# Seven moves in a hand-written order: three accumulating GpSimd transfers later, four other pieces earlier, and four sums of the last chunk on other engines

## The chip, the cores and the metric

The kernel runs on one core of a Trainium2 chip. The number that counts is the device time of one execution in microseconds (us). Before the change three runs took 835.11, 837.05 and 841.11 us, with a median of 837.05 us.

## What is computed

Attention with a causal window of 64 positions over 8 batches, 8 heads, 576 positions and 64 values a head; its output is the input of a gated network without a bias:

```python
scores = (q @ k.T) / 8, only where 0 <= pos_q - pos_k < 64
x = softmax(scores) @ v                 # 4608 tokens x 512
h = x @ w_in                            # 512 -> 2048
g = h * erf(softplus(h))
out = g @ w_out                         # 2048 -> 512, float32
```

## The kernel before

The 4608 tokens are 36 units of 128 for the attention and 18 chunks of 256 for the network. Everything stays on one core, and stages of several units and chunks overlap: while chunk c is in its second product, chunk c+1 or c+2 is in its first, and later units are in the attention.

**Order.** No scheduler decides anything. A string, PLAN, lists tokens such as `B:17:6:0:v`; a loop at the end of the function calls one small function for each token, and every engine gets its instructions in the order of the tokens. The last letter of many tokens says which engine does the piece: `v` VectorE (DVE), `a` ScalarE (ACT), `g` GpSimd (POOL), `d` an accumulating transfer that GpSimd issues. So moving a token moves its instructions on one engine's queue alone, and the others meet it through semaphores.

**The second product from chunk 7 on** is made of seven products of quadrants in place of eight. The gated values y of a chunk lie in two tiles (y_107 and y_108 in the order below), two quadrants in each. The products are called m = 1, 4, 2, 5, 6, 3, 7. The tokens that the change touches, and those beside them:

- `S:c:m` (part_sum, L949 as a transfer, L951 on VectorE) adds one quadrant to another, 128x1024 float32. `S:c:3:d` adds the quadrant of m = 6 to the quadrant of m = 3, both in y_108, by a transfer of 512 KB.
- `A:c:m:h` (part_hi, L585) casts half h of a quadrant to float16, and `B:c:m:h` (part_lo, L944) writes what the cast lost: float32 quadrant less float16 cast, again as float16. Four buffers serve all products in turn, so a cast waits until the matmuls of an earlier product have read its buffer.
- `P:c:m:h` (8 matmuls, L965) multiplies the cast by both float16 parts of the weights, and `Q:c:m:h` (4 matmuls, L965) multiplies the rest from B.
- `K:c:k` (first_out, L412 on ACT, L414 on DVE) scales a PSUM bank into the output row, `J:c:k` (more_out, L985 and L982 on DVE) adds another bank to it. The banks are then written again by the next P.
- `ph:u:p` (L585) and `r:u:p` (L552) make the same two parts of the attention's exponentials; `m:u:p` (L510) masks scores and takes their maximum; `nb` (L517), `n` (normalize, L573 to L575), `dc` (L750) and `gn` (L756, L758) are small.
- `C` (L831) adds PSUM to the hidden values, `E` copies PSUM (L583 or L585), `M` (L815) are the seven products of the first layer.

Of the kernel before, what the change touches and what calls it, by code (L numbers as in the profile page):

```python
# [18 lines left out]
B, H, S, D = 8, 8, 576, 64  # L19
# [3 lines left out]
P = 128  # L23
# [251 lines left out]
)  # L275

# [800 lines left out]
```

## Time and profile before

| | us |
|---|---|
| median of 3 runs | 837.05 (835.11 to 841.11) |
| the profiled execution | 835.41 |
| its span | 833.3 |
| TensorE busy | 807.2 (97%) |
| VectorE busy | 731.7 (88%) |
| ScalarE busy | 629.7 (76%) |
| GpSimd busy | 358.9 (43%) |
| granted TensorE clock, mean | 0.997 |

Busy time counts an instruction from its start to its end, so that an instruction which is held up in the middle counts as busy all the while. The queue of an engine is in order: what waits holds back all that is behind it. [...]

### The profile page before, as it was taken

How to read it: one execution, taken by the hardware profiler on the slowest of the kernel's cores; microseconds unless marked ns; L12 is line 12 of the kernel's file. 1: busy time of each engine (PE TensorE's matmuls, PEld its weight loads, DVE VectorE, ACT ScalarE, POOL GpSimd, SP SyncE). 2: the span in 40 equal slices, each digit the busy share in tenths (PEclk: the TensorE clock that was granted, in tenths of full speed). 3: DMA queues.
4: the chain of work that ended last, by engine and by line, in shares of the span. 5: the costliest groups of instructions: out<-in, count | busy, mean ns of one | idle time of the engine just before them, and what ended most of it. 6: DMA issues, size and time to landing. Idle time of an engine off the chain costs nothing.

```text
span 833.3 us, 26816 instructions
## 1 busy us (share of the span) xinstructions
PE 807.2 (97%) x11358; PEld 675.1 (81%) x11358; DVE 731.7 (88%) x1629; ACT 629.7 (76%) x962; POOL 358.9 (43%) x366
## 2 busy tenths in 40 slices
PE   7899999999999999999999999999998999999996
PEld 7787767566777667667989999999997989899995
DVE  5899999999989998889898899999898888896775
ACT  3799999987878988887778676767786687565482
POOL 1242363424445562822446736283724461523233
PEclk9999999999999999999999999999999999999998
DMA  9974594571486566451746775937476534412222
GB/s 348 360 287 145 149 260 105 121 170 51 104 180 127 144 126 158 121 135 33 137 89 128 178 141 98 212 85 141 98 123 145 111 78 85 74 41 61 52 53 51
DMA packets 148808, 110.40 MB, mean 132 GB/s; under 512 B 123472, under 2 KB 123856, under 8 KB 148688
## 3 DMA queue, kind: packets, MB, share of 16 engines
q1 hardware_dynamic: 145808, 98.60, 48.4%
q0 software_dynamic: 2736, 9.96, 6.4%
q8 instruction: 89, 1.46, 0.8%
q14 instruction: 31, 0.25, 0.1%
q10 hardware_dynamic: 144, 0.13, 0.0%
HBM read 59.64 MB, written 9.44 MB: 83 GB/s over the span
## 4 chain that ended last, share of the span: by engine, by line
PE 64%; DVE 21%; ACT 6%; issue 4%; DMA 3%; POOL 1%; DVEq 0%; SPq 0%; POOLq 0%; ACTq 0%
PE hp L815 27%; PE o L965 15%; PE o L877 12%; PE s L499 3%; PE av L565 3%; PE hp L771 2%; DVE h L944 2%; DVE y L951 1%; DMA y<-y 1%; DVE sm L510 1%; ACT y L839 1%; DVE y L853 1%; DVE h L831 1%; DMA arena<-w_out 1%; PE o L1004 1%
## 5 line engine op out<-in xcount | busy, mean ns | idle before, releaser
L965 PEld LDWEIGHTS <-h 128*128 128x128 f16 x1632 | 156.5, 98 | 27.1 <-DVE h L944 5.5
L815 PE MATMUL hp<-arena,w 128*128 128x128 f16 x2688 | 161.9, 219 | 0.0
L815 PEld LDWEIGHTS <-w 128*128 128x128 f16 x2688 | 154.6, 98 | 6.5 <-issue 2.1
L815 PE MATMUL hp<-arena 128*128 128x128 f16 x2016 | 120.0, 219 | 0.3 <-DVE h L831 0.2
L815 PEld LDWEIGHTS <-arena 128*128 128x128 f16 x2016 | 114.8, 98 | 4.1 <-issue 1.4
L965 PE MATMUL o<-w,h 128*128 128x256 f16 x912 | 109.6, 273 | 2.4 <-DVE ob L985 0.7
L583 ACT ACTIVATE h<-hp 128x512 f32<-128x512 f32 x104 | 60.6, 585 | 42.8 <-PE hp L815 34.7
L771 PE MATMUL hp<-arena,w 128*128 128x256 f16 (+1 forms) x960 | 89.2, 251 | 2.2 <-DVE w L419 1.6
L771 PEld LDWEIGHTS <-w 128*128 128x128 f16 x960 | 77.7, 98 | 13.2 <-DVE w L419 2.1
L839 ACT ACTIVATE y<-h,c 128x1024 f32<-128x1024 f32 x72 | 80.1, 1142 | 10.2 <-DVE h L831 8.7
L583 ACT ACTIVATE h<-y 128x512 f16<-128x512 f32 x79 | 46.8, 623 | 43.2 <-PE o L965 12.8
L944 DVE TENSOR_TENSOR h<-y,h 128x512 f16<-128x512 f32 x95 | 74.1, 797 | 4.3 <-ACT h L583 2.4
L877 PE MATMUL o<-w,gh 128*128 128x512 f16 x320 | 75.0, 379 | 0.2 <-ACT arena L412 0.2
L944 POOL TENSOR_TENSOR h<-y,h 128x512 f16<-128x512 f32 x41 | 53.3, 1324 | 50.6 <-DVE h L585 16.0
L846 ACT ACTIVATE y<-y 128x1024 f32<-128x1024 f32 x72 | 74.4, 1052 | 0.4
L831 DVE TENSOR_TENSOR h<-hp,h 128x512 f32<-128x512 f32 x84 | 57.6, 686 | 18.9 <-PE hp L815 16.4
L851 DVE SCALAR_TENSOR_TENSOR y<-h,small,y 128x1024 f32<-128x1024 f32 x44 | 58.0, 1331 | 4.7 <-ACT y L846 4.5
L965 PE MATMUL o<-spare,h 128*128 128x256 f16 x460 | 55.7, 274 | 3.2 <-DVE h L944 3.2
L877 PEld LDWEIGHTS <-gh 128*128 128x128 f16 x320 | 30.2, 98 | 32.9 <-issue 0.5
L846 ACT ACT_TABLE_LOAD x39 | 50.0, 1283 | 0.7
L499 PE MATMUL s<-kr,qr 64*64 64x128 f32 x1152 | 41.2, 280 | 6.6 <-DMA kr<-k_in 4.7
L949 POOL DMA_DIRECT2D y<-y x19 | 17.2, 903 | 69.1 <-DVE h L585 14.8
(256 smaller groups left out, 1661.4 us busy)
## 6 DMA issues: line engine op xcount, KB each, us to landing
vr<-v_in SPq DMA_DIRECT2D x36, 520.0 KB, 4.3
kr<-k_in SPq DMA_DIRECT2D x36, 384.0 KB, 4.0
y<-y POOLq DMA_DIRECT2D x19, 512.0 KB, 5.1
qr<-q_in SPq DMA_DIRECT2D x36, 256.0 KB, 3.8
out<-ob SPq DMA_DIRECT2D x33, 256.0 KB, 2.9
w<-w_in SPq DMA_DIRECT2D x4, 1024.0 KB, 8.6
arena<-w_in SPq DMA_DIRECT2D x4, 1024.0 KB, 9.2
arena<-w_out SPq DMA_DIRECT2D x4, 1024.0 KB, 6.0
```

The source lines that it names most:

```text
L499: nc.tensor.matmul(sps[par][t, i, :], qx[rows, i, t], kx[rows, i, W * blk:W * blk + P], start=n == 0, stop=n == len(terms) - 1)
L565: nc.tensor.matmul(avp[t, par, j, :], pt[a][ab(u)][:, HP * par + j, t], vs[b][ab(u)][:, blk, 2 * j + par, :], start=a + b == 0, stop=a == 1)
L583: nc.scalar.activation(dst, src, AF.Copy)
L771: nc.tensor.matmul(hps[pc % 2][:, f, at_t], w1[a][hf][:, cc, fs], xt[b][c % 2][:, cc:2 * NCC:NCC, :][:, at_x, :], start=(n == 0), stop=(n ...
L815: nc.tensor.matmul(bank[:, q, f, :], left(m, a, 2 * hf + q)[:, cc, f * P:(f + 1) * P], xt[b][c % 2][:, slot + cc, :], start=m in (1, 2, 5) ...
L831: nc.vector.tensor_tensor(dst, bank_view(1), dst, op=ALU.add)
L839: nc.scalar.activation(at(yb, g, n), at(hb, g, n), AF.Softplus, scale=st_c[g][:, n:n + 1])
L846: nc.scalar.activation(y, y, AF.Erf)
L851: nc.vector.scalar_tensor_tensor(y, at(hb, g, n), gain(g, n), y, op0=ALU.mult, op1=ALU.mult)
L877: nc.tensor.matmul(ops[j], a[:, f // 2, j, f % 2, :], w2[b][:, hf * GF + n * GF // 2 + f, :], start=n == 0 and f == 0 and a is gh and b == ...
L944: eng_of(eng).tensor_tensor(lo, quadrant(m)[:, 512 * h:512 * (h + 1)], hi, op=ALU.subtract)
L965: nc.tensor.matmul(dst, a[:, at_f], right(m, n, 2 * h + f // 2)[:, f % 2], start=False, stop=f == 3 and (a is lo or n == 1), skip_group_ch ...
```

## The change

Seven edits of PLAN; no function changes. Before, the three transfers stand right after an earlier piece of GpSimd; now they stand behind later ones.

1. Chunk 7: `A:7:3:1:v A:7:3:0:v` come ahead of `n:21`, and `B:7:7:1:v` ahead of `B:7:3:0:v`, all on VectorE.
2. Chunk 8: `J:8:0` (VectorE) comes ahead of `m:26:1`.
3. Chunk 12: `S:12:3:d` (GpSimd) comes after `B:12:6:0:g` and `r:32:0:g`.
4. Chunk 14: `S:14:3:d` comes after `A:14:6:1:g`, `dc:34:g` and `ph:35:1:g`.
5. Chunk 16: `S:16:3:d` comes after `B:16:5:0:g`.
6. Chunk 17, engines: `B:17:6:0`, `B:17:5:0` and `B:17:5:1` go from GpSimd to VectorE, `B:17:7:1` from VectorE to GpSimd.
7. Chunk 17, order: `B:17:5:1` comes ahead of `K:17:1` and `J:17:0`.

Two of the changed lines, those of chunk 17 (the others only move tokens, as listed):

```diff
-    "B:17:6:1:v P:17:6:1 A:17:5:0:a B:17:6:0:g A:17:7:1:a P:17:6:0 B:17:7:1:v Q:17:6:1 B:17:5:0:g Q:17:6:0 P:17:5:0 "
-    "K:17:1:a J:17:0 B:17:5:1:g P:17:7:1 B:17:7:0:g Q:17:7:1 Q:17:5:0 Q:17:5:1 P:17:7:0 K:17:2:a A:17:3:1:v A:17:3:0:a "
+    "B:17:6:1:v P:17:6:1 A:17:5:0:a B:17:6:0:v A:17:7:1:a P:17:6:0 B:17:7:1:g Q:17:6:1 B:17:5:0:v Q:17:6:0 P:17:5:0 "
+    "B:17:5:1:v K:17:1:a J:17:0 P:17:7:1 B:17:7:0:g Q:17:7:1 Q:17:5:0 Q:17:5:1 P:17:7:0 K:17:2:a A:17:3:1:v A:17:3:0:a "
```

The order of TensorE, ScalarE and SyncE is the same in both kernels; only VectorE and GpSimd differ. In the rows below, h_106, kr_85 and kr_86 are buffers that B writes, y_107 and y_108 the gated values, o_117 a PSUM bank, ob the output row.

VectorE at the end, chunk 17 (the L951 row is `S:17:6`, the L985 row `J:17:0`, the L944 rows are B):

```order
 L951 TENSOR_TENSOR y_108<-y_108,y_107 128x1024
 L585 CAST h_106<-y_108 128x512
-L944 TENSOR_TENSOR h_106<-y_108,h_106 128x512
-L944 TENSOR_TENSOR kr_86<-y_107,kr_86 128x512
+L944 TENSOR_TENSOR h_106<-y_108,h_106 128x512 x2
+L944 TENSOR_TENSOR h_106<-y_107,h_106 128x512 x2
 L985 SCALAR_TENSOR_TENSOR ob<-o_117,sg,ob 128x256
 L585 CAST h_106<-y_108 128x512
```

Between `S:17:6` and `J:17:0` VectorE had two sums B and has four. GpSimd at the same place, behind its last two transfers:

```order
 L949 DMA y_107<-y_107 128x1024
 L949 DMA y_108<-y_108 128x1024
-L944 TENSOR_TENSOR h_106<-y_108,h_106 128x512
-L944 TENSOR_TENSOR h_106<-y_107,h_106 128x512 x2
+L944 TENSOR_TENSOR kr_86<-y_107,kr_86 128x512
 L944 TENSOR_TENSOR kr_85<-y_107,kr_85 128x512
 L944 TENSOR_TENSOR h_106<-y_108,h_106 128x512
```

Behind the last transfer GpSimd had four sums in a row and has two, and then a last one that belongs to m = 3. GpSimd in chunk 12 (the L949 row that moves is `S:12:3`, L552 is `r:32:0`, the L585 row is `A:12:7:0`):

```order
 L944 TENSOR_TENSOR h_106<-y_107,h_106 128x512
 L949 DMA y_107<-y_107 128x1024
-L944 TENSOR_TENSOR h_106<-y_108,h_106 128x512
-L949 DMA y_108<-y_108 128x1024
-L944 TENSOR_TENSOR h_106<-y_108,h_106 128x512
+L944 TENSOR_TENSOR h_106<-y_108,h_106 128x512 x2
 L552 TENSOR_TENSOR p_0_98<-sm_95,p_0_97 128x512
+L949 DMA y_108<-y_108 128x1024
 L585 CAST h_106<-y_107 128x512
```

The transfer has gone behind one sum B and one sum of the attention.

## Rows read from the trace of the kernel before

**Rows 1.** The page: busy us (share of the span) and instructions of each engine.
```profile
PE 807.2 (97%) x11358; PEld 675.1 (81%) x11358; DVE 731.7 (88%) x1629; ACT 629.7 (76%) x962; POOL 358.9 (43%) x366
```

**Rows 2.** Timeline of chunk 17: start us, us, engine, line, instruction; idle time before it.
```profile
815.44 0.88 POOL L949 DMA_DIRECT2D y<-y  x1 [8.98 <-DVE h L585]
816.00 3.72 POOL L944 TENSOR_TENSOR h<-y,h 128x512 f16<-128x512 f32 x3
816.74 4.63 DVE L944 TENSOR_TENSOR kr<-y,kr 128x512 f16<-128x512 f32 x1 [0.64 <-ACT kr L583]
818.21 0.47 ACT L412 ACTIVATE ob<-o,sg 128x256 f32<-128x256 f32 x1 [1.50 <-PE o L965]
819.34 1.48 POOL L944 TENSOR_TENSOR kr<-y,kr 128x512 f16<-128x512 f32 x1
821.83 2.62 PE L965 MATMUL o<-w,kr 128*128 128x256 f16 x12 [2.78 <-DVE ob L985]
```

**Rows 3.** Line L944: instructions, minimum/median/maximum ns, first and last start.
```profile
L944 DVE TENSOR_TENSOR h<-y,h x95: 671/685/2403, 405.2 to 827.9; 128x512 f16<-128x512 f32 x95
L944 POOL TENSOR_TENSOR h<-y,h x41: 1144/1163/2135, 404.1 to 827.2; 128x512 f16<-128x512 f32 x41
```

**Rows 4.** Stretches: busy time of each engine, then granted clock, DMA share, GB/s.
```profile
821.80:825.40 3.60, 3.57 (x18) 2.50 (x18) 0.31 (x1) 0.00 (x0) 0.00 (x0) 0.53 0.00 0
628.20:630.10 1.90, 0.09 (x2) 0.05 (x2) 1.90 (x11) 0.02 (x1) 0.06 (x1) 1.00 0.98 195
```

**Rows 5.** Timeline at 467 and at 474 us: single meetings of the two engines.
```profile
467.61 2.18 DVE L419 SCALAR_TENSOR_TENSOR vs<-vr,csc,vs 128x1024 f16<-128x1024 f32 x1
474.58 2.24 POOL L552 TENSOR_TENSOR p<-qk,p 128x512 f16<-128x512 f32 x1 [0.56 <-ACT p L583]
```

**Rows 6.** Timeline of chunk 12.
```profile
624.55 0.86 POOL L949 DMA_DIRECT2D y<-y  x1 [3.97 <-DVE h L944]
625.16 3.40 DVE L585 CAST p<-sm 128x512 f16<-128x512 f32 x1
627.38 0.89 POOL L585 CAST h<-y 128x512 f16<-128x512 f32 x1
630.06 1.05 PE L965 MATMUL o<-spare,h 128*128 128x256 f16 x8 [1.81 <-DVE h L944]
634.24 0.63 ACT L583 ACTIVATE h<-y 128x512 f16<-128x512 f32 x1 [0.66 <-PE o L965]
```

**Rows 7.** Timeline of chunk 14.
```profile
708.17 0.88 POOL L949 DMA_DIRECT2D y<-y  x1 [4.03 <-DVE y L951]
708.61 2.40 DVE L944 TENSOR_TENSOR h<-y,h 128x512 f16<-128x512 f32 x1
709.63 0.83 POOL L585 CAST p<-qk 128x512 f16<-128x512 f32 x1
711.07 3.78 PE L965 MATMUL o<-spare,h 128*128 128x256 f16 x33 [0.61 <-DVE h L944]
712.80 0.63 ACT L583 ACTIVATE h<-y 128x512 f16<-128x512 f32 x1 [4.38 <-DMA y<-y]
715.21 0.63 ACT L583 ACTIVATE h<-y 128x512 f16<-128x512 f32 x1 [0.62 <-PE o L965]
```

**Rows 8.** Timeline of chunk 16.
```profile
787.89 2.07 DVE L944 TENSOR_TENSOR vr<-y,vr 128x512 f16<-128x512 f32 x1
790.02 1.48 PE L965 MATMUL o<-spare,vr 128*128 128x256 f16 x12 [0.34 <-DVE vr L944]
796.00 0.61 POOL L585 CAST vr<-y 128x512 f16<-128x512 f32 x1 [2.02 <-PE o L965]
```

**Rows 9.** Timeline of chunks 7 and 8.
```profile
424.01 1.92 PE L965 MATMUL o<-w,h 128*128 128x256 f16 x16 [0.51 <-DVE h L585]
465.78 5.40 PE L965 MATMUL o<-w,h 128*128 128x256 f16 x48 [0.66 <-DVE ob L985]
```

**Rows 10.** Line L949: from issue to landing of the 19 transfers.
```profile
DMA to landing us min/median/max: 4.5/5.1/7.2
```

42 rows, old and new, of the table PLAN are left out of this document.

## Prediction

> **What bounds the kernel now.** I first read the busy times: TensorE is busy 97% of the span, VectorE 88%, GpSimd 43% [rows 1]. So a change pays only where TensorE stands still, and there is little of that. Next I read the timeline at each of the seven places, for two things: an idle time in front of a TensorE row, and a VectorE row much longer than its kind. They come together. A sum B takes VectorE 0.685 us at the median and GpSimd 1.163 [rows 3]. In chunk 17 one took VectorE 4.63 us, and in that time GpSimd ran four sums without a gap, from 816.00 to 820.82; VectorE ended 0.55 us after GpSimd did [rows 2]. The same is seen in chunk 12 (a cast of 3.40 us; GpSimd ends at 628.27, the cast at 628.56) [rows 6], and sums of 2.40 in chunk 14 [rows 7] and 2.07 in chunk 16 [rows 8] are of the same sort. Each time GpSimd had just issued a transfer for which it had waited, so that the pieces behind it were ready and came in a row. I read this as one resource that either engine holds while it works from SBUF to SBUF, and that GpSimd, once it runs in a row, does not hand over.
>
> Single meetings show the rest [rows 5]. At 467.61 VectorE needed 2.18 us: one GpSimd piece was ahead of it, and then it went on. At 474.58 GpSimd's sum came while VectorE was at work; it took 2.24 us, 1.1 more than a median sum [rows 3]. So whichever engine comes second waits for the piece of the other, and I take it that a waiting GpSimd gets in at the next boundary between two VectorE instructions.
>
> **Chunk 17.** TensorE stands still for 2.78 us, from 819.05, until `J:17:0` has read its bank [rows 2]. It restarts at a granted clock of 0.53 (mean over 3.6 us) [rows 4]. At full clock the same work takes 3.6 × 0.53 = 1.9, so the clock costs another 1.7 us. In chunk 12 an idle time of 1.81 [rows 6] was followed by no fall: its stretch has 1.00 [rows 4].
>
> Now VectorE has four sums and then `J:17:0`. The first ends at 816.1 as before (816.74 less the 0.64 idle) [rows 2]. `B:17:6:0` and `B:17:5:0` follow at 0.6 to 0.7 each until 817.3. The cast for `B:17:7:1` is done at 816.7, since that sum started then [rows 2]; now GpSimd has it, waits at 817.3 and gets in, with `B:17:7:0` right behind. At the pace of the four, (820.82 - 816.00)/4 = 1.2 each, GpSimd is through at 819.7. Then come `B:17:5:1` until 820.3 and `J:17:0` until 820.8 (0.46, from 821.37 to 821.83 before). TensorE goes on at 820.8 in place of 821.83: **1.0 us**. Its idle time is then 1.75, below the 1.81 that cost no clock, so the **1.7** come back too. The bounds: at best `B:17:5:1` gets in ahead of GpSimd and `J:17:0` waits only for `K:17:1` (ends 818.68) [rows 2]; TensorE goes on at 819.2, 2.6 + 1.7 = 4.3. At worst one more sum stands behind GpSimd's two and the clock falls all the same: 0.4. I take 2.7, because the meeting at 474 us is the nearest case. The transfer of this chunk is issued as early as before, so what reads it is not later.
>
> **Chunk 12.** GpSimd's two sums ahead of the transfer start no later than they did, and VectorE's cast stands behind two pieces instead of three: the third took 0.89, from 627.38 [rows 6]. VectorE is free earlier by **0.9 us**, and the 1.81 in front of TensorE at 630.06 shrinks by as much [rows 6]. Bounds: 0 (the third piece comes as early as before) and 1.81. The transfer is issued near 627.3 in place of 624.55. Its reader on ScalarE started at 634.24 [rows 6], so 633.3 now; with the median landing of 5.1 the data are there at 632.4, with the longest, 7.2, at 634.5 [rows 10]. I cost it at nothing; at worst ScalarE waits 1.2.
>
> **Chunk 14.** The three pieces that go ahead of the transfer started some 0.6 behind it (as 816.00 behind 815.44 [rows 2]), at 708.8, and the third ended at 710.46 [rows 7]. The first needs the sum `S:14:6` as the transfer does, so they now start when the transfer did or a little later, at 708.2 to 708.4, and end at 709.7, with less in their way. The VectorE sum behind them then ends at 710.7 in place of 711.0: **0.3** of TensorE's 0.61 [rows 7]. The transfer is issued at 709.7 in place of 708.17, and here its reader already waits for it, 4.38 us until 712.80 [rows 7]. That row moves to 714.3. The cast after it on ScalarE waited for TensorE itself, until 715.21 [rows 7], and takes up most of the 1.5; I add 0 for it. Bounds for the whole place: -3.0 (worked out below) and +0.6.
>
> **Chunk 16.** `B:16:5:0` comes the 0.6 of an issue earlier, and VectorE's sum is through as much earlier (0 to 1.4, its whole excess over 0.68). TensorE waited 0.34 for it [rows 8]: **0.35**. The transfer is issued near 788.6; with the longest landing it is there at 795.8 [rows 10], and its reader on GpSimd started at 796.00 [rows 8]. Covered.
>
> **Chunks 7 and 8.** The casts ahead of `n:21` end TensorE's wait of 0.51 [rows 9]. `n:21` reads PSUM, and I expect it to go on beside a GpSimd sum; VectorE gains less than TensorE: **0.4** (0 to 0.51). `J:8:0` ahead of four masked maxima ends the wait of 0.66 [rows 9], but takes no work off VectorE, and ScalarE's exponentials behind the maxima come 0.5 later. I count half: **0.3** (-0.5 to 0.66).
>
> **Sum.** 2.7 + 0.9 + 0.3 + 0.35 + 0.4 + 0.3 = 4.95 us. Against the profiled execution (835.41, of which 833.3 span) that gives 830.5; it lies 1.6 below the median of the runs, which gives 832.1. I put the forecast between them, at **831**. What a place gains can be lost later where VectorE sets the pace; therefore the idle times themselves (2.78 + 1.7 + 1.81 + 0.61 + 0.34 + 0.51 + 0.66 = 8.4) are the end of the range and not the forecast.
>
> [...]
>
> **Rivals.** A measurement of this kernel can tell about 1% from no change: below 828.7 is faster, above 845.4 slower.
>
> *Given up after every instruction.* The pieces arrive at new moments, and VectorE gets in behind the first GpSimd piece everywhere. Chunk 17: GpSimd from 817.3 to 818.5, then a sum and `J:17:0`, 819.6, so 2.2 + 1.7 = 3.9. Chunk 12: the cast waits for one sum, 1.8. Chunk 14 0.6, chunk 16 0.35, chunks 7 and 8 1.2. Together 7.9, or 827.5 to 829.2; I take 828. For it: 467 us [rows 5]. Against it: the long waits over several pieces.
>
> *Little is left.* The clock falls in chunk 17 in spite of the shorter wait (1.75 is hardly under 1.81), so 1.0 there, and of the rest only 1.0 lasts until the end, because VectorE at 88% sets the pace in between. 2.0 less: 834. It decides where VectorE has no pause between one place and the next.
>
> *The late transfer of chunk 14 holds ScalarE: slower.* Issued at 709.7, it holds the cast of 715.21 as soon as landing takes over 4.2 (715.21 less two ScalarE pieces of 0.63, less 709.7) [rows 7]. With the longest landing, 7.2 [rows 10], its reader starts at 716.9 and that cast at 718.2, 3.0 late, and TensorE waits as long for the product behind it. If besides only 1.0 of chunk 17 is gained and nothing else, the kernel takes 837 + 2 = 839. Against it: this landing took 4.6 (708.17 to 712.80) [rows 7], and of 19 the median is 5.1 [rows 10].
>
> [...]
>
> **Numbers.** Chances: the forecast 0.52, "after every instruction" 0.22, "little is left" 0.18, "late transfer" 0.08. The range of 826.5 to 836.5 takes in the first three with the spread of single runs about them, and leaves out the fourth and the ends. Faster by over 1%: half of the first rival and a little of the forecast, 0.13. Slower by over 1%: 0.02. The same within 1%: 0.85.
>
> **What would show it.** In the profile after: the sums of chunk 17 on VectorE at 0.7 except one of about 3 us; a wait in front of TensorE there of under 1.8, with a clock of 1.00 behind it; in chunk 12 a cast of about 2.5 in place of 3.40; in chunk 14 a reader some 1.5 later than before. I am wrong if a VectorE row of 4 us stands in another place, if the granted clock falls again, or if the waits of TensorE are shorter at the seven places and longer at others.

## The result, and the profile after

The changed kernel took **827.75 us** (median of 20 runs, 825.32 to 838.74); the kernel before, in 20 runs on the same chips, 838.08 (833.57 to 846.24). The ratio is 0.990, with a 95% interval of 0.9868 to 0.9932: 1.0% faster, a little more than the 0.7% that was forecast (831 against 837.05). Here and below the ratio leaves out the few runs in a slower state and is not the quotient of the two medians. The first rival had said 828. The profiled execution took 828.04, of which 826.1 is its span; before it was 835.41 and 833.3.

The busy times, the row that answers to [rows 1]:

```profile
PE 805.6 (98%) x11358; PEld 674.7 (82%) x11358; DVE 725.4 (88%) x1631; ACT 629.4 (76%) x962; POOL 355.1 (43%) x364
```

The work is the same; VectorE is busy for 6.3 us less although it runs two instructions more. What it lost was waiting inside its instructions. Line L944, that of the sums B, says so (minimum/median/maximum ns), beside [rows 3]:

```profile
L944 DVE TENSOR_TENSOR h<-y,h x98: 671/686/1647, 407.2 to 820.7; 128x512 f16<-128x512 f32 x98
L944 POOL TENSOR_TENSOR h<-y,h x38: 1147/1159/1976, 406.1 to 819.9; 128x512 f16<-128x512 f32 x38
```

No sum B on VectorE takes over 1.65 us now; before there were some of 2.07, 2.40 and 4.63, and a cast of 3.40.

**Where the time went.** TensorE runs the same 11,358 matmuls in the same order in both kernels, so the two traces can be laid beside each other: the start of the same matmul, after minus before. No edit bears on TensorE before 424 us, and there the changed one was already 1.97 us late (a group of 24 matmuls starts at 423.97 in place of 422.00); that is one execution against another. At the end it was 7.25 us early. Each step is this difference just behind a place less the one just ahead of it:

| Place | Forecast | Step measured |
|---|---|---|
| Chunk 7 | 0.4 | 0.91 |
| Chunk 8 | 0.3 | 0.82, of which 0.78 is given back by 504 us |
| Chunk 12 | 0.9 | 1.97 |
| Chunk 14 | 0.3 | 0.77 at 711 us, 0.36 at 716, 0.61 at 722, less 0.11 given back at 725: 1.63 |
| Chunk 16 | 0.35 | 0.50 |
| Chunk 17, the wait | 1.0 | 2.52 |
| Chunk 17, the clock | 1.7 | 1.67 |
| Sum | 4.95 | 9.2 (from 1.97 late to 7.25 early) |

The spans of the two traces differ by 7.2 us, that is 9.2 less the 1.97. The medians of the runs differ by 10.3 and the lowest times by 8.3; single times scatter by more than such a difference, for a reason that runs 9 and 10 show.

Chunk 17, the timeline, to be read beside [rows 2]:

```profile
812.34 3.46 DVE L944 TENSOR_TENSOR h<-y,h 128x512 f16<-128x512 f32 x4
812.36 0.88 POOL L949 DMA_DIRECT2D y<-y  x1 [8.92 <-DVE h L585]
...
813.76 3.05 POOL L944 TENSOR_TENSOR kr<-y,kr 128x512 f16<-128x512 f32 x2 [0.52 <-ACT kr L583]
...
815.72 0.47 DVE L985 SCALAR_TENSOR_TENSOR ob<-o,sg,ob 128x256 f32<-128x256 f32 x1
816.25 0.93 PE L965 MATMUL o<-w,kr 128*128 128x256 f16 x7 [0.27 <-DVE ob L985]
```

VectorE's four sums take 3.46 us in all, and the longest of them 1.65 (the maximum in the rows of L944): it met one sum of GpSimd and went on between GpSimd's two. These end at 816.81, 1.0 us after VectorE's row. GpSimd has a pause of 0.52 between the transfer and the first sum, since that sum now waits for a cast on ScalarE. TensorE waits 0.27 in place of 2.78. The stretch behind it (busy time of PE, PEld, DVE, ACT, POOL, then TensorE's granted clock as a share of full speed, DMA share, GB/s), beside [rows 4]:

```profile
816.20:822.60 6.40, 6.27 (x56) 5.37 (x55) 2.07 (x4) 1.21 (x2) 1.77 (x2) 1.00 0.20 66
```

The granted clock stays at 1.00, where it had been 0.53.

Chunk 12, beside [rows 6]:

```profile
626.08 1.16 POOL L944 TENSOR_TENSOR h<-y,h 128x512 f16<-128x512 f32 x1 [4.44 <-ACT h L583]
626.21 1.31 DVE L585 CAST p<-sm 128x512 f16<-128x512 f32 x1
...
627.21 1.33 POOL L552 TENSOR_TENSOR p<-sm,p 128x512 f16<-128x512 f32 x1
...
628.49 0.86 POOL L949 DMA_DIRECT2D y<-y  x1
...
630.94 0.50 PE L965 MATMUL o<-spare,h 128*128 128x256 f16 x3 [0.75 <-DVE h L944]
```

The cast meets the first of two GpSimd sums and gets in between them: 1.31 us in place of 3.40. The wait of 1.81 is gone; a wait of 0.74 stood behind it before as well, where there is one of 0.75 now.

Chunk 14, beside [rows 7]:

```profile
708.15 0.68 DVE L944 TENSOR_TENSOR h<-y,h 128x512 f16<-128x512 f32 x1
...
709.39 0.88 POOL L949 DMA_DIRECT2D y<-y  x1
...
714.02 0.63 ACT L583 ACTIVATE h<-y 128x512 f16<-128x512 f32 x1 [6.47 <-DVE h L585]
```

The sum of 2.40 us now takes 0.68. The transfer is issued 1.2 us later than before and its reader on ScalarE starts 1.2 later; TensorE stands still nowhere for it.

In chunk 16 VectorE's sum went from 2.07 [rows 8] to 1.45. In chunk 7 the 0.51 in front of TensorE is gone [rows 9], and so is a second wait that the forecast did not look at, 0.24 for a VectorE sum B at 426.18. Chunk 8 has a new short wait of ScalarE on VectorE, whose row that feeds the exponentials stands behind a GpSimd sum:

```profile
466.47 1.16 POOL L944 TENSOR_TENSOR h<-y,h 128x512 f16<-128x512 f32 x1 [1.61 <-ACT h L583]
...
466.68 0.98 DVE L517 TENSOR_SCALAR small<-small 128x8 f32<-128x8 f32 x1
...
467.69 0.40 ACT L543 ACTIVATE sm<-sm,small 128x128 f32<-128x128 f32 x1 [1.29 <-DVE small L517]
```

That this wait is what gave the 0.78 back was not tried.

### The profile page after: what moved, and what is told of

Read it like the earlier page. It is cut to its first block, busy times and chain, and to the rows that moved or that the text cites. A ratio compares the mean times of both kernels' runs of the same rounds, so it can differ in the third digit from the quotient of the medians.

```text
span 826.1 us, 26816 instructions
## 1 busy us (share of the span) xinstructions
PE 805.6 (98%) x11358; PEld 674.7 (82%) x11358; DVE 725.4 (88%) x1631; ACT 629.4 (76%) x962; POOL 355.1 (43%) x364
## 5 line engine op out<-in xcount | busy, mean ns | idle before, releaser
L839 ACT ACTIVATE y<-h,c 128x1024 f32<-128x1024 f32 x72 | 80.0, 1141 | 10.3 <-DVE h L831 9.4
L944 DVE TENSOR_TENSOR h<-y,h 128x512 f16<-128x512 f32 x98 | 74.7, 782 | 4.0 <-ACT h L583 2.8
L944 POOL TENSOR_TENSOR h<-y,h 128x512 f16<-128x512 f32 x38 | 48.5, 1280 | 49.8 <-ACT h L583 19.8
L543 ACT ACTIVATE sm<-sm,small 128x128 f32<-128x128 f32 x124 | 39.0, 389 | 6.7 <-POOL small L517 5.1
```

What stands on the lines that cost most here:

```text
L543: nc.scalar.activation(s[:, j, :], s[:, j, :], AF.Exp, bias=nmx[u % 2][:, HP * par + j:HP * par + j + 1], scale=0.125)
L839: nc.scalar.activation(at(yb, g, n), at(hb, g, n), AF.Softplus, scale=st_c[g][:, n:n + 1])
L944: eng_of(eng).tensor_tensor(lo, quadrant(m)[:, 512 * h:512 * (h + 1)], hi, op=ALU.subtract)
```

## The experiments

The two theories ahead of the runs: by the forecast, GpSimd never hands over once it runs in a row; by the other, the engines take turns after each instruction, except for GpSimd's pieces straight behind a transfer that GpSimd itself issued. The second came from the trace of before: its four VectorE rows that took over 1.1 us more than the median of their kind (3.40, 2.40, 2.07, 4.63 [rows 2, 6 to 8]) are four that stood behind such a transfer. The 2.07 of chunk 16 fits both theories, though: behind that transfer GpSimd ran a single sum, from 787.96 to 789.41, and VectorE's ended 0.55 later. Lines in the variants of the whole kernel are ten lower than in the profiles above (L934 for L944, L939 for L949).

**1. The transfer of chunk 17 moved, nothing else.** The kernel before, with the transfer behind the three sums:

```diff
-P:17:5:1 S:17:3:d K:17:0:a ... J:17:0 B:17:5:1:g P:17:7:1
+P:17:5:1 K:17:0:a ... J:17:0 B:17:5:1:g S:17:3:d P:17:7:1
```

> The kernel before, with one token moved: the last transfer S:17:3 goes behind GpSimd's three sums B:17:6:0, B:17:5:0 and B:17:5:1 (only B:17:7:0 stays behind it); all sums stay on their engines. Theory 1 (the one recorded: GpSimd, once it runs in a row, does not hand over): VectorE's B:17:7:1 still waits for the row, a VectorE row of 3 us or more, TensorE's wait in front of P:17:7:1 over 1.5 us. Theory 2 (VectorE gets in after each GpSimd piece, except in a row straight behind a transfer): a VectorE row of at most 1.7 us, a wait of TensorE under 0.7 us, clock 1.00 behind it, and the TensorE matmuls from there some 4 us earlier, relative to the place before, than in the kernel before. The time is then about 4 us lower, 0.5%.

It took 839.78 us against 835.72 (ratio 1.0013, interval 0.9967 to 1.0059): no gain. The timeline:

```profile
824.94 4.01 POOL L934 TENSOR_TENSOR h<-y,h 128x512 f16<-128x512 f32 x3 [9.30 <-ACT h L573]
...
825.92 0.90 DVE L934 TENSOR_TENSOR kr<-y,kr 128x512 f16<-128x512 f32 x1 [0.66 <-ACT kr L573]
...
828.40 1.47 PE L955 MATMUL o<-w,kr 128*128 128x256 f16 x12 [0.21 <-DVE ob L975]
...
834.05 0.39 PE L955 MATMUL o<-w,h 128*128 128x256 f16 x2 [1.99 <-DVE h L575]
```

The same sum that had taken 4.63 us takes 0.90, beside the same three GpSimd sums, and the wait of 2.78 is 0.21: without the transfer in front of them the engines take turns. About 4.2 us were won there (2.57 of the wait, 1.67 of the clock), but the transfer's data came late, TensorE stood 1.99 us for them and the clock fell once more (granted 0.90 in the mean from 832 to 836 us; from the start of the last 24 matmuls to the end of the span 7.75 us, 6.28 in run 5, some 1.5 more); some 3.5 were given back. The second theory held there (0.90 for 4.63), the expected gain in time is a miss.

**2. The changed kernel with a sum behind the transfer again.**

```diff
-S:17:3:d K:17:0:a ... J:17:0 P:17:7:1 B:17:7:0:g Q:17:7:1
+S:17:3:d B:17:7:0:g K:17:0:a ... J:17:0 P:17:7:1 Q:17:7:1
```

> The changed kernel with one token moved: B:17:7:0 (its cast long done) stands straight behind the last transfer, ahead of B:17:7:1. Theory 2: the two GpSimd sums run in a row from about 0.56 us behind the issue, and one VectorE sum waits for both: a VectorE row of about 2.5 to 3 us where the changed kernel has 1.65 at most. Rival (every GpSimd piece hands over, the transfer has no part in it): no VectorE row there over 1.7 us.

One run took 829.12 us. VectorE's four sums and GpSimd's two in chunk 17:

```profile
L934 DVE TENSOR_TENSOR h<-y,h x4: 677/686/3146, 811.7 to 816.0; 128x512 f16<-128x512 f32 x4
```

```profile
812.29 2.60 POOL L934 TENSOR_TENSOR kr<-y,kr 128x512 f16<-128x512 f32 x2
...
815.51 1.48 PE L955 MATMUL o<-spare,h 128*128 128x256 f16 x12 [1.49 <-DVE h L934]
```

Here GpSimd has no pause behind the transfer, and one VectorE sum waits for both sums (3.15 us; 1.65 in the changed kernel). TensorE now stands 1.49 us for the sum, and by the starts of the same matmuls it is 1.60 us later behind this place than the changed kernel, as measured from ahead of it.

**3. The two engines alone.** A small kernel (it leaves out the whole computation): VectorE runs 12 sums while GpSimd runs four, with something different in front of GpSimd's; each case three times. Four of its six cases:

```diff
+gsum(0, early); gsum(1..3, ga)                               # plain
+gpsimd.dma_start(big0, big1, accum_op=add); gsum(0..3, ga)   # transfer in front
+gpsimd.dma_start(big0, big1); gsum(0..3, ga)                 # plain copy in front
+gpsimd.dma_start(..., accum_op=add); gsum(0, late); gsum(1..3, ga)   # and a wait of ~2 us
```

> A kernel of its own that leaves out the whole computation and measures only how the two engines meet. VectorE runs 12 sums of the form of B (128x512, float32 less float32 to float16) in a row; beside it GpSimd runs four such sums, in six cases, three times each: nothing in front of them; an accumulating transfer of 512 KB from GpSimd straight in front; a plain copy from GpSimd straight in front; the copy issued by SyncE; an accumulating transfer and then a wait of about 2 us before the four; one sum and then the transfer. Theory 1: in all cases with four sums one VectorE sum waits for all of them, 4 us or more. Theory 2: only in the cases with a GpSimd transfer straight in front (accumulating or plain) is there a VectorE row of 4 us or more; in the others no row over 1.9 us, several of about 1.8 in turn. Theory 3 (only accumulating transfers do it): the plain copy behaves as without a transfer.

The durations of VectorE's sums (L33) in the first round of the first three cases, in this order, and in the fourth the first sum of GpSimd (L36):

```profile
L33 DVE TENSOR_TENSOR vo<-va,vb x12: 678/680/1744, 8.1 to 18.7; 128x512 f16<-128x512 f32 x12
...
L33 DVE TENSOR_TENSOR vo<-va,vb x12: 677/678/5767, 20.4 to 32.1; 128x512 f16<-128x512 f32 x12
...
L33 DVE TENSOR_TENSOR vo<-va,vb x12: 676/678/5948, 33.8 to 45.7; 128x512 f16<-128x512 f32 x12
...
L36 POOL TENSOR_TENSOR go<-late,gb x1: 5159/5159/5159, 63.1 to 63.1; 128x512 f16<-128x512 f32 x1
```

Plain, no VectorE sum takes over 1.76 us in any round: a meeting costs it 1.08 at most over the 0.68 of a sum that meets nothing, less than one GpSimd sum (1.25 behind VectorE's row in the fourth case). Straight behind the accumulating transfer one VectorE sum takes 5.77 (5.68 and 5.72 in the other two rounds): it waits for all four. A plain copy issued by GpSimd did the same once in three (5.95; 1.76 and 1.80 in the other rounds). The two cases not shown are as the plain one: behind a copy issued by SyncE, and with the transfer behind GpSimd's sum in place of ahead of it, no VectorE sum takes over 1.76. In the fourth case it is the other way round: GpSimd's sum took 5.16 and ended 1.1 us after VectorE had no more work (VectorE's 12 sums took 0.69 at most). That was expected by neither theory.

Chunks 12 and 17 after the change are like the plain case (1.74 in the round shown): the cast took 1.31 and the longest sum 1.65. In the 5.77, several instructions of GpSimd ran while one of VectorE waited, in the 5.16 several of VectorE while one of GpSimd did; what lets an engine keep on like this, the run does not show.

**4. Is it the wait that costs the clock?** The kernel before, with 24 matmuls that nobody reads put into TensorE's wait:

```diff
-J:17:0 B:17:5:1:g P:17:7:1
+J:17:0 B:17:5:1:g kb:24 P:17:7:1
```

> The kernel before, with 24 matmuls of 128 columns into a hidden bank that is no longer read, put in front of P:17:7:1 on TensorE; they do no part of the computation and fill some 2.4 of the 2.78 us for which TensorE stands still. If the fall of the clock follows from the standstill, the clock stays at 1.00 behind it and the TensorE work from P:17:7:1 to the last matmul (7.96 us before) takes 6.3 us or less, 1.65 us gained at the end. If the clock falls for another reason, it is 0.5 again for 3.4 us and nothing is gained.

```profile
818.58 1.55 PE L998 MATMUL hp<-one,ident 128*128 128x128 bf16 x24
...
821.50 0.71 PE L955 MATMUL o<-w,kr 128*128 128x256 f16 x5 [1.37 <-DVE ob L975]
```

The wait is 1.37 and a filled stretch; the granted clock is 1.00 throughout, and the work from there to the end of the last matmul takes 6.27 us in place of 7.94: 1.67. So the fall belongs to the standstill, and its price is 1.67 us, as the forecast had it. One run took 833.47.

**5 and 6. Chunk 17 alone, and all but chunk 17.** The kernel before with the edits of chunk 17, and the changed kernel without them:

```diff
-B:17:6:0:g ... B:17:7:1:v ... B:17:5:0:g ... J:17:0 B:17:5:1:g
+B:17:6:0:v ... B:17:7:1:g ... B:17:5:0:v ... B:17:5:1:v K:17:1:a J:17:0
```

> The kernel before with the two edits of chunk 17 alone (engines of four sums, B:17:5:1 ahead of J:17:0). Theory 2 (VectorE gets in after each GpSimd piece unless the row follows straight behind a transfer): no VectorE row over 1.7 us there, a wait in front of P:17:7:1 of about 0.3, no fall of the clock, and the end 4.2 us earlier relative to the place before it: ratio near 0.995. Theory 1 (the sizes recorded): 2.7 us, ratio 0.997, a wait of about 1.75.

> The changed kernel without the two edits of chunk 17: chunks 7, 8, 12, 14 and 16 as changed. Theory 2: VectorE rows of at most 1.5 us in chunks 12, 14 and 16, TensorE's matmuls 0.9 earlier behind chunk 7, 1.9 behind chunk 12, 1.7 behind chunk 14, 0.4 behind chunk 16, nothing left of chunk 8; together 4.9 us before chunk 17, where the row of 4.6 us and the fall of the clock are as in the kernel before. Ratio near 0.994. Theory 1 (the sizes recorded): 2.25 us, ratio 0.997.

Chunk 17 alone: 834.01 against 838.68, ratio 0.9957 (0.9919 to 0.9996). All but chunk 17: 830.75, ratio 0.9897 (0.9859 to 0.9936). TensorE's waits in the two, first chunk 17 alone, then all but it:

```profile
629.45 1.05 PE L955 MATMUL o<-spare,h 128*128 128x256 f16 x8 [1.81 <-DVE h L934]
...
819.33 1.47 PE L955 MATMUL o<-w,kr 128*128 128x256 f16 x12 [0.28 <-DVE ob L975]
```

```profile
817.17 4.60 DVE L934 TENSOR_TENSOR kr<-y,kr 128x512 f16<-128x512 f32 x1 [0.68 <-ACT kr L573]
...
822.22 2.72 PE L955 MATMUL o<-w,kr 128*128 128x256 f16 x12 [2.78 <-DVE ob L975]
```

Each half removes its own waits and leaves the other's. In the traces chunk 17 is worth 2.50 and 1.67 for the clock, 4.2 in all; 0.59 was lost just ahead of it, where ScalarE and VectorE waited longer for an earlier transfer (7.3 us to landing, 6.7 in the trace of before). The others show the steps of the table again (0.91, 0.82 with 0.45 given back, 1.97, 1.63, 0.50), 5.4 in all. In time the halves are 4.7 and 7.9 by the medians, together more than the 10.3 of the whole change, and all but chunk 17 did better than the 0.994 that was expected. The 5.4 is 0.9936, the very end of that half's interval; why its runs were faster still stays open.

**7. Can more be had?** The changed kernel with two VectorE pieces earlier:

```diff
-B:12:6:1:v P:12:6:1 ... pk:33:2:v Q:12:6:1 B:12:5:1:v lk:35
+B:12:6:1:v B:12:5:1:v P:12:6:1 ... pk:33:2:v Q:12:6:1 lk:35
-B:17:5:1:v K:17:1:a J:17:0 P:17:7:1
+K:17:1:a J:17:0 B:17:5:1:v P:17:7:1
```

> The changed kernel with two more moves on VectorE: B:12:5:1 straight behind B:12:6:1 (ahead of C:26:2 and a maximum), and J:17:0 ahead of B:17:5:1. If the two waits that the changed kernel still has there (0.75 at 630.2 us and 0.27 at 816.0) hang on these two instructions, both go to 0.1 or less and the kernel takes 1.0 us less than the changed one, ratio to the kernel before near 0.988. Rival: C:26:2, now 0.7 later, holds ScalarE's softplus and TensorE waits later instead; then nothing is gained.

831.86 us (826.36 to 837.79), ratio to before 0.9891 (0.9849 to 0.9933): not to be told from the changed kernel, and the 1.0 us that was expected did not come. The 0.75 of chunk 12 became 0.39, but 0.48 was given back by 638 us. In chunk 17 `J:17:0` now waits for ScalarE, which waits for TensorE:

```profile
814.71 0.48 DVE L975 SCALAR_TENSOR_TENSOR ob<-o,sg,ob 128x256 f32<-128x256 f32 x1 [1.40 <-ACT ob L402]
...
815.25 1.47 PE L955 MATMUL o<-w,kr 128*128 128x256 f16 x12 [0.21 <-DVE ob L975]
```

0.21 in place of 0.27: nothing is left there.

**8. What makes the row behind a transfer.** The small kernel again (it leaves out the whole computation): 18 sums on VectorE, and on GpSimd two sums that are released by the last of k casts on ScalarE (0.65 us each), with and without a transfer in front.

```diff
+scalar.activation(late, mark) x k;  gpsimd.dma_start(..., accum_op=add) or nothing;  gsum(0..1, late);  vsum(0..17)
```

> A kernel of its own that leaves out the whole computation: 18 VectorE sums in a row beside two GpSimd sums, which ScalarE releases after 1, 2, 3, 4, 6 or 9 casts of 0.6 us, with and without an accumulating GpSimd transfer in front (2 times each). Theory 2a: the transfer matters only if the GpSimd sums follow without a pause; then one VectorE sum waits for both (over 2.5 us), and with a pause the engines take turns (rows of 1.7 to 1.8). Theory 2b (from the case with a pause in the first kernel of this kind, where a GpSimd sum behind a transfer took 5.16 us): behind a transfer the engines do not take turns at all; the one that is at work keeps on until it pauses, so that with a pause it is GpSimd's first sum that waits, until VectorE's row ends. Without a transfer they take turns in both theories.

VectorE's sums for k = 1 with and without the transfer, and GpSimd's for k = 4 with it:

```profile
L33 DVE TENSOR_TENSOR vo<-va,vb x18: 676/677/3608, 8.1 to 21.2; 128x512 f16<-128x512 f32 x18
...
L33 DVE TENSOR_TENSOR vo<-va,vb x18: 676/678/1751, 22.9 to 35.3; 128x512 f16<-128x512 f32 x18
...
L36 POOL TENSOR_TENSOR go<-late,gb x2: 1252/4942/8632, 96.4 to 105.0; 128x512 f16<-128x512 f32 x2
```

With k = 1 GpSimd's first sum starts 0.8 us after the start of the transfer's issue (0.6 in the second round), and one VectorE sum waits for both sums (3.61, and 3.24); without the transfer they take turns. With k = 2, where the sum starts 1.0 after it (0.9), and with k = 3 they take turns in either case: a short pause behind the transfer is enough. With k = 4, 6 and 9 GpSimd arrives 3.3 us or more after VectorE's row began, and its first sum ends 1.1 or 1.2 us behind the end of that row (with k = 4 it takes 8.63 us with the transfer and 8.71 without it). So the second surprise of run 3 has nothing to do with the transfer.

**9 and 10. The two terms that were too small, undone one by one.** The changed kernel with the transfer of chunk 14, and of chunk 12, back where it was:

```diff
-B:14:5:0:v Q:14:2:1 ... ph:35:1:g S:14:3:d P:14:5:1
+S:14:3:d B:14:5:0:v Q:14:2:1 ... ph:35:1:g P:14:5:1
-B:12:5:0:v Q:12:2:1 ... r:32:0:g S:12:3:d C:26:2
+S:12:3:d B:12:5:0:v Q:12:2:1 ... r:32:0:g C:26:2
```

> The changed kernel with the edit of chunk 14 undone: the accumulating transfer S:14:3 stands again straight behind S:14:6, ahead of the three pieces of GpSimd. Theory (behind a transfer GpSimd's ready pieces run as one row): the VectorE sum there takes 2.2 to 2.6 us again in place of 0.7, TensorE stands about 0.6 us in front of the matmul that reads it and some 0.4 twice within the next 11 us, and the same matmul of TensorE starts 1.7 us later than in the changed kernel from there on. Rival (the size in the forecast): only the first wait belongs to this edit, the two later ones hung on the order further ahead; 0.3 to 0.6 us later. Second rival (the transfer that was moved back costs its reader): the cast of chunk 14 on ScalarE that reads it had been 1.2 us late, so undoing the edit gains something at 715 us; under 0.3 us later in all.

> The changed kernel with the edit of chunk 12 undone: the accumulating transfer S:12:3 stands again ahead of GpSimd's sums B:12:6:0 and r:32:0. Theory: VectorE's cast waits for the row behind the transfer, 3.2 to 3.6 us in place of 1.31, TensorE stands 1.6 to 2.0 us in front of the matmul that the changed kernel started without a wait, and is 1.9 us later than in the changed kernel behind it. Rival (the forecast's rule, by which the cast stands behind two pieces in the one order and three in the other): 0.9 us later.

Chunk 14 undone:

```profile
717.08 0.87 POOL L939 DMA_DIRECT2D y<-y  x1 [4.03 <-DVE y L941]
717.52 2.40 DVE L934 TENSOR_TENSOR h<-y,h 128x512 f16<-128x512 f32 x1
...
719.98 3.78 PE L955 MATMUL o<-spare,h 128*128 128x256 f16 x33 [0.60 <-DVE h L934]
...
724.63 0.96 PE L555 MATMUL av<-vs,pt 128*64 128x65 f16 x47 [0.40 <-DVE vs L409]
...
730.94 0.28 PE L955 MATMUL o<-w,h 128*128 128x256 f16 x1 [0.44 <-POOL h L934]
```

The sum is back at 2.40, and with it three waits of TensorE, not one. Against the changed kernel the same matmuls start 0.77, then 0.36, then 0.61 us later, and 0.11 comes back behind them: 1.63. Chunk 12 undone:

```profile
628.61 3.40 DVE L575 CAST p<-sm 128x512 f16<-128x512 f32 x1
...
633.51 1.05 PE L955 MATMUL o<-spare,h 128*128 128x256 f16 x8 [1.81 <-DVE h L934]
```

1.97 us later. Both as the theory had it; the rivals fall.

The single times of these two (839.33 and 832.31) say little: in both, TensorE also stood still near 510 us, long before the place of the edit. For chunk 14 undone:

```profile
502.31 0.87 POOL L939 DMA_DIRECT2D y<-y  x1 [5.21 <-DVE cdiag L444]
...
516.06 0.63 ACT L573 ACTIVATE h<-y 128x512 f16<-128x512 f32 x1 [7.00 <-DMA y<-y]
...
517.31 1.01 PE L955 MATMUL o<-w,h 128*128 128x256 f16 x4 [7.01 <-ACT ob L402]
```

That transfer landed after 13.7 us. Four of the ten traces of the whole kernel have such a standstill there (4.68, 3.49, 7.01 and 3.15 us; longest landings of 11.9, 10.1, 13.7 and 10.3), and the other six, those of before and of the changed kernel among them, have none (at most 7.3). Run 1, whose program is that of before up to chunk 17, has it too, so it comes and goes from one execution to another. The clock falls behind it: in run 6, with a wait of 3.49, the 32 matmuls behind took 5.32 us, where 48 took 5.40 in the trace of before. In all it adds up to 10 us: the span of run 9 is 11.4 longer than that of the changed kernel (837.5 and 826.1), of which the edit has 1.63. So steps of a microsecond are read here from the starts of the same matmul, not from single times.

## Why the prediction came out as it did

The sign was right, and so was the place where the time was sought: waits inside VectorE's instructions. The sizes were not: 9.2 us came in the traces for the 4.95 of the sum. The time lies in the range all the same, because the range was made wide enough for the first rival too, and the measured 827.75 is that rival's 828, not the forecast's 831. That much is luck. The terms were too small, mostly because of one step.

**The step that failed** is "GpSimd, once it runs in a row, does not hand over". Where a row was seen not to hand over, it followed a GpSimd transfer without a pause (runs 1 to 3 and 8 to 10). The change does not only shorten such rows, it takes the pieces out from behind the transfer (chunks 12, 14 and 16) or puts a pause between (chunk 17). What happened there is the first rival, "given up after every instruction", with 828 and a chance of 0.22. The forecast saw that the long rows stood behind a transfer, and took it as the reason that the pieces were ready, not as part of the mechanism. That one resource lies behind the waits is the author's reading; the runs show the waits alone (in run 3 5.77 us for VectorE, 5.16 for GpSimd).

Nor does every ready row behind a transfer hold VectorE off. In the kernel before, at 408 us, GpSimd's first piece starts 0.79 us behind the issue, the next follows at once, and VectorE's sum gets in between the two:

```profile
407.77 1.05 POOL L949 DMA_DIRECT2D y<-y  x1 [2.21 <-DVE y L951]
408.56 1.46 POOL L907 TENSOR_TENSOR misc<-w 128x512 f32<-128x512 f16 x1
...
409.40 1.18 DVE L944 TENSOR_TENSOR h<-y,h 128x512 f16<-128x512 f32 x1
410.10 1.50 POOL L907 TENSOR_TENSOR misc<-misc,w 128x512 f32<-128x512 f32 x1
```

- **Chunk 17.** `B:17:5:1` was put behind both sums of GpSimd; it got in behind one. 2.52 in place of 1.0; the rival's 2.2 is nearer.
- **The clock.** 1.67, here and in run 4, for 1.7. The standstill that remains is 0.27, so a standstill of 1.75 was not put to the test there; in run 1 the clock did fall behind 1.99 us (granted 0.90 in the mean from 832 to 836).
- **Chunk 12.** 1.97 (the same in run 10) in place of 0.9: the cast waits for part of one piece, not for two. The rival had 1.8.
- **Chunk 14** was mis-sized most: 1.63 (the same in run 9) in place of 0.3, outside the bound of 0.6. That counted only the first wait behind the 2.40 us sum. VectorE has no pause from there to 718.9 us, so the same lateness showed again as a wait of 0.40 for VectorE at 715.7; a third, of 0.44 at 722.0, was for a GpSimd sum. Run 9 shows that both belong to the edit; how the third hangs on it was not traced.
- **Chunk 16.** 0.50 for 0.35. Here a single GpSimd piece stood behind the transfer, so the failed step has no part in it.
- **Chunk 7.** 0.91 for 0.4, also outside its bound of 0.51, which left out the second wait of 0.24. `n:21` did go on beside a GpSimd sum: its longest row took 0.69 us from 425.23, beside a sum of 1.23 from 424.68, and none of the 36 rows of that line (L575) in the trace of before took over 0.693. The edit was not undone by itself.
- **Chunk 8.** Nothing net for 0.3. The doubt that ScalarE's exponentials come later showed up (1.29); that it is the cause stays open.
- **The later transfers** cost nothing in chunks 12, 14 and 16, as said, and "late transfer" did not come. Run 1 shows the price of such lateness where there is no slack: 3.5 us in chunk 17, the one place where the change leaves the transfer where it was.
- **"Little is left"** fell: but for chunk 8, what a place gained lasted to the end.

Of what was to show it, the wait under 1.8 with a clock of 1.00 behind it came, and the later reader in chunk 14 (1.2 for 1.5); a VectorE sum of about 3 us in chunk 17 (1.65) and a cast of about 2.5 in chunk 12 (1.31) did not.

One row was not what the forecast took it for. That 1.81 us cost no clock it read from the stretch of the standstill itself [rows 4]; the standstill of chunk 17 has 1.00 as well. What tells is the stretch behind it, 0.53 in chunk 17 [rows 4] and 1.00 in chunk 12, so the conclusion holds:

```profile
819.00:821.80 2.80, 0.04 (x1) 0.00 (x0) 2.80 (x3) 0.00 (x0) 1.82 (x2) 1.00 0.13 23
...
630.10:634.00 3.90, 3.16 (x28) 2.60 (x29) 3.87 (x9) 3.05 (x3) 0.27 (x1) 1.00 1.20 212
```

## What to carry to other kernels

Look for VectorE rows several times as long as their kind (here 2.07 to 4.63 us for a sum of 0.685), and at what stands in front of GpSimd's row beside them: if GpSimd has just issued a transfer, its ready pieces can go through as a block (four in chunk 17 before, and in run 3 beside the 5.77). Put such a transfer behind the pieces (chunk 12: 3.40 became 1.31), or give the first piece behind it something to wait for (chunk 17: 0.52 us, and 4.63 became 1.65); but first see how much slack the transfer's reader has (in run 1 none: 3.5 us). And follow a late VectorE row for as long as that engine has no pause: the waits that it causes are further on as well (in chunk 14 0.36 and 0.61 behind the first 0.77).

## What was not expected of the hardware

- Straight behind a transfer issued by GpSimd, up to four GpSimd sums ran while one VectorE sum waited for all: 5.68 to 5.77 us, three times of three, with an accumulating transfer, 4.63 in the kernel. A pause was enough to end this: in the small kernels, with the first sum 0.9 us or more after the start of the accumulating transfer's issue they took turns, with 0.8 or less not. In the kernel before they took turns with 0.79 as well, so the time alone does not decide it; what does stays open.
- GpSimd can be held off as well: where VectorE had run sums without a pause for 3.3 us or more, a GpSimd sum did not end until 1.1 or 1.2 us after VectorE's row, and took 5.2 to 8.7 us; with 2.7 us they still took turns. No row of the kernel before or after shows this (their longest sums on GpSimd in line L944 take 2.14 and 1.98).
- One accumulating transfer of 512 KB landed after 7.3 us or less in six traces and after 10.1 to 13.7 in four, at the same place of the program.
